# Earlier weight fetches, later scaling of omega, and bfloat16 norm matmuls in a random-feature attention with a bilinear network behind it

## The chip, the cores and the metric

The kernel runs on one core of one Trainium2 chip. The metric is device time in microseconds; the kernel before took 866.14 us (median of 3 runs, 863.68 to 867.47). A profiled execution of the same program is read below.

## The reference

q, k and v have 8 batches, 8 heads, 576 tokens and 64 columns; omega is 128 x 64. With x scaled by 64 to the power -1/4, the feature map is

```python
proj = einsum('bhsd,md->bhsm', x, omega)
h = proj - sum(x * x, -1) / 2
phi = exp(h - max(h, -1)) / sqrt(128)
```

Then kv = sum over tokens of phi(k) times v, z = sum of phi(k), and the attention's output is phi(q) kv / (phi(q) z + 1e-6). Its 4608 tokens of 512 columns go through out = (((x w1) * (x w2)) w3) w_out, with w1 and w2 of 512 x 1024, w3 of 1024 x 1024 and w_out of 1024 x 512. The four weights arrive as float64.

## The kernel before, in words

The tokens are cut into 36 chunks of 128. For a chunk of k, `features` (L258) projects it with omega on TensorE (PE) into two PSUM banks, VectorE (DVE) takes the maximum over the features (L295), ScalarE (ACT) makes the exponentials, and `in_parts` splits the result into two float16 halves. The first 9 chunks of k and the first 5 of q are projected as float32, straight from the loaded chunk and omega ("whole"); later chunks are first scaled by a power of two and split into float16 halves, and are multiplied with omega's own scaled halves. `kv_batch` sums features times v over the chunks of a batch; `q_chunk` and `q_attend` do the same for q, with a transpose by DMA between; `gate` and `project_out` are the network, with w3 w_out multiplied out once beforehand into one matrix W (`W_block`, L562).

Powers of two come from a sum of squares over a whole tile. ACT squares and sums each row; `power_of_two` (L162) adds the 128 rows by a matmul with a matrix of ones, so that every row holds the sum, and DVE takes the exponent. This matmul is called a norm here. Norms stand for omega ("om"), for each step's chunk of q and of k together ("q_k", later "q" alone), for each batch of v and for W. Omega's norm and split (L200 to L206) come at the head of the program, behind omega's two loads. The `om` halves and `unom` that they make are read from chunk 9 of k and chunk 5 of q on.

A weight goes in units through five stages: `fetch` (a DMA of 1 MB, issued on ACT's queue, L486) into one of three raw buffers of the arena, `magnitude` (ACT takes the absolute value of the high words, L494) into one of two buffers, `bits` (four DVE instructions, L500 to L504, which make float32 from float64), and, by kind, a product of PE with a copy by ACT, or a sum of magnitudes. `ORDER` gives the units: "ooWWWW11a22b..." are two units of w_out, four products of w3 with it, then w1 and w2. The stages of successive units are skewed by one tick each.

What stands where is written out as a plan of slots: each slot takes `PER[t]` ticks of the weight pipeline, one unit of the network's queue, and the functions put there by `put(slot, rank, fn)`, by rank; chunk i of q and chunk i + 5 of k begin at slot `begin[i]`, three slots each, from slot 3 on. So k's chunk 0 is projected in slot 3, behind three ticks in slot 0 and one each in slots 1 and 3. The planner of the tile framework takes this order as priority: on each engine and queue it issues what is ready by its own estimate, earlier traced work first; each engine then executes its own list in order. Loads of k, q and v and the stores stand in SyncE's (SP's) queue, weight fetches in ACT's.

Of the kernel before, what the change touches and what calls it, by code (L numbers as in the profile page):

```python
# [9 lines left out]
F32 = mybir.dt.float32  # L10
F16 = mybir.dt.float16
BF16 = mybir.dt.bfloat16
I32 = mybir.dt.int32
U32 = mybir.dt.uint32
AF = mybir.ActivationFunctionType
ALU = mybir.AluOpType
# [3 lines left out]
P = 128  # L20
# [32 lines left out]
EARLY = 6  # L53
KV_LAG = 5
K_LATE = 8
RAW64_BUFS = 3
O_BUFS = 2
RAW_BUFS = 2
# [10 lines left out]
def tile_favor_attention_then_bilinear_ffn(  # L69
# [19 lines left out]
    nc = tc.nc  # L89
# [12 lines left out]
    SCALE = 1.0 / math.sqrt(math.sqrt(D))  # L102
    TOK = GROUP * P

    const = ctx.enter_context(tc.tile_pool(name="const", bufs=1))
# [16 lines left out]
    make_identity(nc, ident)  # L122
    ones_bf = const.tile([P, P], BF16, name="ones_bf")
    nc.vector.memset(ones_bf, 1.0)
    ones = const.tile([P, P], F32, name="ones")
    nc.vector.memset(ones, 1.0)
    ln_e = const.tile([P, 1], F32, name="ln_e")
    nc.vector.memset(ln_e, 15 * math.log(2.0))

# [22 lines left out]
    def square_sum(out, src, name, pre=1.0):  # L152

        n = src.shape[1] * (src.shape[2] if len(src.shape) > 2 else 1)
        junk = at.tile([P, 512], BF16, tag="junk", name=f"junk_{name}", bufs=1)
        r0, rows = 0, src.shape[0]
        dst = junk[r0 : r0 + rows, 0:n]
        if len(src.shape) > 2:
            dst = dst.rearrange("p (i j) -> p i j", i=src.shape[1])
        nc.scalar.activation(dst, src, AF.Square, scale=pre, accum_out=out)  # L160

    def power_of_two(cols, n, name, pre=1.0, add=False, bufs=4):  # L162

        bank = bank_m(f"norm_{name}")
        nc.tensor.matmul(bank[:, 0:n], ones, cols, start=True, stop=True)
        t = bank[:, 0:n]
        if add:
            total = small("total")
            nc.vector.tensor_reduce(total, t, AX.X, ALU.add)
            t, n = total, 1  # L170

        q = bank[:, 16 : 16 + n]
        p = bank[:, 32 : 32 + n]

        nc.vector.tensor_scalar(
            q.bitcast(I32), t.bitcast(I32), 24, 23, ALU.logical_shift_right, ALU.logical_shift_left
        )
        nc.vector.tensor_scalar(p, q, 2.0**50 / pre, 2.0**-77 / pre, ALU.mult, ALU.max)
        s = small(f"s{n}_{bufs}", n, bufs=bufs)
        nc.vector.reciprocal(s, p)  # L180
        return p, s
# [13 lines left out]
    om_raw = Wb[:, 0, 0:M]  # L195
    nc.sync.dma_start(om_raw[0:D], omT)
    nc.sync.dma_start(om_raw[D:P], omT)
    om = const.tile([P, 2, M], F16, name="om")
    om_sq = const.tile([P, 1], F32, name="om_sq")
    square_sum(om_sq, om_raw, "om")  # L200
    pom, som = power_of_two(om_sq, 1, "om")
    nc.scalar.mul(om[:, 0], om_raw, som)
    nc.vector.scalar_tensor_tensor(om[:, 1], om_raw, som, om[:, 0], ALU.mult, ALU.subtract)

    unom = const.tile([P, 1], F32, name="unom")
    nc.vector.tensor_scalar_mul(unom, pom, SCALE)  # L206

    def chunks_of(b):

# [5 lines left out]
    def load(src, c, name):  # L215
        t = at.tile([P, NP, P], F32, tag=f"{name}raw", name=f"{name}raw_{c}", bufs=RAW_BUFS)
        nc.sync.dma_start(t, src[c])
        raws[name, c] = t
# [39 lines left out]
    def features(c, name):  # L258


        if whole(c, name):
            raw, es = raws.pop((name, c)), SCALE
        else:
            hl, es = hls.pop((name, c))
        pg = banks(f"{name}pj_{c}").rearrange("p g (i m) -> p g i m", m=M)
        pj = pg.rearrange("p g i m -> p (g i) m")

        def project(first=None):
            for i in range(NP):
                if first is not None:  # L270
                    for g in range(2):
                        nc.tensor.matmul(pg[:, g, i], ident, first(g * NP + i), start=True, stop=False)
                if whole(c, name):
                    for g in range(2):
                        d = slice(g * D, (g + 1) * D)
                        nc.tensor.matmul(  # L276
                            pg[:, g, i], raw[d, i], om_raw[d], start=first is None, stop=True
                        )
                    continue
                for n, (x, y) in enumerate(PASSES):  # L280
                    for g in range(2):
                        d = slice(g * D, (g + 1) * D)
                        nc.tensor.matmul(  # L283
                            pg[:, g, i],
                            hl[d, x, i],
                            om[d, y],
                            start=first is None and n == 0,
                            stop=n == len(PASSES) - 1,
                        )

        project()
        if whole(c, name) and c + 2 < NCH:
            load(srcs[name], c + 2, name)
        nm = small("nm", H)
        nc.vector.tensor_reduce(nm, pj, AX.X, ALU.max, negate=True)  # L295
        e = at.tile([P, H, M], F32, tag="e", name=f"{name}e_{c}", bufs=2)
        kind = pick(DK if name == "k" else DQ, c)
        if kind == "2":

            project(lambda h: nm[:, h : h + 1].broadcast_to([P, M]))  # L300
            nc.scalar.activation(e, pj, AF.Exp, scale=es, bias=ln_e)
        elif kind == "1":

            nc.vector.tensor_scalar(nm, nm, es, 15 * math.log(2.0), ALU.mult, ALU.add)
            for h in range(H):
                nc.scalar.activation(e[:, h], pj[:, h], AF.Exp, scale=es, bias=nm[:, h : h + 1])
        else:
            nc.vector.tensor_tensor(e, pj, nm.unsqueeze(2).broadcast_to([P, H, M]), ALU.add)  # L308
            nc.scalar.activation(e, e, AF.Exp, scale=es, bias=ln_e)  # L309
        return e  # L310
# [9 lines left out]
    ek, vhl, vraw, pv, kvs = {}, {}, {}, {}, {}  # L320

    def k_chunk(c):
        e = features(c, "k")
        ek[c] = at.tile([P, 2, H, M], F16, tag="ek", name=f"ek_{c}", bufs=EK_BUFS)
        in_parts(ek[c], e, pick(EH, c), pick(EL, c))

    def v_load(c):
        vraw[c] = at.tile([P, H, D], F32, tag="vraw", name=f"vraw_{c}", bufs=VRAW_BUFS)
        nc.sync.dma_start(vraw[c], v[c])

    vam, sv = {}, {}

# [135 lines left out]
        return free.pop(0)  # L468

    left = {}  # L470

    def used(at):

# [4 lines left out]
    def from_float64(new, src, name):  # L478

        st = {}  # L480

        def fetch():
            at = st["at"] = raw_at.pop(0)
            raw = arena[:, at : at + 4].bitcast(U32).rearrange("p b i -> p (b i)")

            nc.scalar.dma_start(raw.rearrange("p (j i) -> p j i", j=src.shape[1]), src)  # L486
            st["raw"] = raw.rearrange("p (i t) -> p i t", t=2)

        def magnitude():

            at = st["mag"] = mag_at.pop(0)
            st["g"] = arena[:, at : at + 2].rearrange("p b i -> p (b i)")
            st["dst"] = new()
            nc.scalar.activation(st["g"], st["raw"][:, :, 1].bitcast(F32), AF.Abs)  # L494

        def bits():
            g = st["g"]
            top, low = st["raw"][:, :, 1], st["raw"][:, :, 0]

            nc.vector.tensor_scalar(g, g, F64_TOP, F64_LEAST, ALU.min, ALU.max)  # L500
            g = g.bitcast(U32)
            nc.vector.tensor_scalar(g, g, 3, 0x3FFFFFFF, ALU.logical_shift_left, ALU.bitwise_and)
            nc.vector.scalar_tensor_tensor(g, top, 0xC0000000, g, ALU.bitwise_and, ALU.bitwise_or)  # L503
            nc.vector.scalar_tensor_tensor(  # L504
                st["dst"].bitcast(U32), low, 29, g, ALU.logical_shift_right, ALU.bitwise_or
            )
            raw_at.append(st["at"])
            mag_at.append(st["mag"])

        return [fetch, magnitude, bits]  # L510
# [203 lines left out]
    units, seen = [], {}  # L714
    for ch in ORDER:
        n = seen.get(ch, 0)
        seen[ch] = n + 1
        st = make[ch](n)
        units.append([None] * 3 + st + [None] if len(st) == 1 else st + [None] * (5 - len(st)))
    behind = sorted(range(5), key=lambda k: -SKEW[k])  # L720
    ticks = [
        [units[t - SKEW[k]][k] for k in behind if 0 <= t - SKEW[k] < len(units) and units[t - SKEW[k]][k]]
# [17 lines left out]
    def put(slot, rank, fn):  # L740
        plan.setdefault(slot, []).append((rank, len(plan[slot]) if slot in plan else 0, fn))
# [65 lines left out]
        step(i)  # L807
    for c in range(2):
        load(kT, c, "k")
    put(begin[-1] - 3, 11, lambda: load(qT, 0, "q"))  # L810
    put(begin[-1] - 2, 11, lambda: load(qT, 1, "q"))
    for t in range(max(plan) + 1):
        n = min(PER[t] if t < len(PER) else 1, len(ticks))
# [9 lines left out]
        n = max([1] + [-(-(k + 1) // max(due[b] - t, 1)) for k, (b, _) in enumerate(v_work)])  # L823
# [43 lines left out]
```

## Time and profile before

| | |
|---|---|
| median of 3 runs | 866.14 us |
| profiled execution, its own time | 866.7 us |
| span in the profile | 865.0 us |
| PE busy | 789.3 us (91%) |
| DVE busy | 594.4 us (69%) |
| ACT busy | 455.0 us (53%) |
| POOL busy | 222.0 us (26%) |
| chain that ended last, by engine | PE 81%, DVE 8%, DMA 4%, ACT 4%, issue 2% |
| mean DMA rate | 102 GB/s |

Busy time is the union of an engine's instructions; PEld is TensorE's weight load, which overlaps PE. The chain is the work followed back from the last instruction, at each step to what released it. A line number is that of the kernel before. The shares are averages over a beginning, in which engines wait for each other, and a long stretch in which PE is full, so they are read by stretch below.

### The profile page before, as it was taken

To read this page: it belongs to the slowest core of one execution; us is meant where nothing else is said; L and a number is where in the kernel's file an instruction comes from. 1 tells how busy PE (TensorE), PEld (TensorE's weight loads), DVE (VectorE), ACT (ScalarE), POOL (GpSimd) and SP (SyncE) were. 2 spreads that over 40 slices of the span, in tenths; PEclk is the share of its full clock that TensorE was granted. 3 is DMA by queue.
4 is the path that set the end of the run, shared out by engine and by line. 5 is a ranking of instruction groups with operands and counts; after the bars stand their busy time and mean duration, and the time that the engine had idled before them with its cause. 6 is when DMAs were issued, how large, how long until landed. Compare 5 with 4: busy or idle time off the path is not lost.

```text
span 865.0 us, 20229 instructions
## 1 busy us (share of the span) xinstructions
PE 789.3 (91%) x8479; PEld 585.1 (68%) x8484; DVE 594.4 (69%) x1066; ACT 455.0 (53%) x813; POOL 222.0 (26%) x220
## 2 busy tenths in 40 slices
PE   2876399489996899999999999999999999999998
PEld 2344255387875777777777777877777777777774
DVE  5778887887879877777877777778777754652200
ACT  2667566758456665655565656555655443322221
POOL 0000010222333433334333334343333342222110
PEclk9996599699998999999999999999999999999999
DMA  8455646432444643644534434335342343332100
GB/s 328 150 191 164 196 129 190 119 59 62 87 112 102 96 115 95 98 75 98 123 86 87 111 98 99 74 89 133 87 87 62 62 80 81 63 62 49 37 14 36
DMA packets 142522, 88.40 MB, mean 102 GB/s; under 512 B 116704, under 2 KB 116832, under 8 KB 142432
## 3 DMA queue, kind: packets, MB, share of 16 engines
q1 hardware_dynamic: 134944, 66.15, 33.7%
q10 hardware_dynamic: 7488, 20.97, 7.3%
q8 instruction: 66, 1.08, 0.5%
q14 instruction: 24, 0.20, 0.1%
HBM read 49.35 MB, written 9.44 MB: 68 GB/s over the span
## 4 chain that ended last, share of the span: by engine, by line
PE 81%; DVE 8%; DMA 4%; ACT 4%; issue 2%; POOL 0%; SPq 0%; ACTq 0%; DVEq 0%
PE ab L636 40%; PE o L665 20%; PE wp L576 7%; PE nu L401 3%; PE kvp L366 3%; PE qpj L283 2%; PE kpj L283 2%; DMA kraw<-kT 1%; DVE nm L295 1%; DMA eqT<-eq 1%; PE wp L574 1%; DMA qraw<-qT 1%; DVE w12b L504 1%; DVE arena L503 1%; PE kpj L276 1%
## 5 line engine op out<-in xcount | busy, mean ns | idle before, releaser
L636 PE MATMUL ab<-xT,w12b 128*128 128x256 f16 (+1 forms) x3840 | 396.0, 263 | 10.4 <-DMA xT<-xhl 7.1
L636 PEld LDWEIGHTS <-w12b 128*128 128x128 f16 x3840 | 342.7, 99 | 51.7 <-issue 9.0
L665 PE MATMUL o<-Wb,arena 128*128 128x512 f16 x864 | 193.6, 379 | 1.1 <-DVE Wb L146 0.6
L651 POOL TENSOR_TENSOR arena<-asb,arena 128x512 f16<-128x512 f32 x72 | 84.5, 1174 | 294.9 <-ACT arena L650 294.4
L665 PEld LDWEIGHTS <-arena 128*128 128x128 f16 x864 | 84.3, 100 | 94.6 <-issue 1.5
L318 POOL TENSOR_TENSOR eq<-qe,eq 128x1024 f16<-128x1024 f32 x34 | 73.9, 2172 | 141.2 <-DVE eq L132 86.8
L646 DVE TENSOR_TENSOR asb<-ab,asb 128x512 f32<-128x512 f32 x72 | 49.4, 687 | 62.9 <-PE ab L636 62.5
L650 ACT CAST arena<-asb 128x512 f16<-128x512 f32 x72 | 44.3, 615 | 85.5 <-DVE asb L646 85.5
L318 POOL TENSOR_TENSOR ek<-ke,ek 128x1024 f16<-128x1024 f32 x28 | 59.7, 2131 | 103.2 <-ACT ek L134 62.2
L576 PE MATMUL wp<-w12b 128*128 128x512 f32 x128 | 60.9, 631 | 13.5 <-DVE w12b L504 13.5
L309 ACT ACTIVATE qe<-qe,ln_e,es 128x1024 f32<-128x1024 f32 x31 | 38.4, 1240 | 47.6 <-DVE qe L308 47.6
L146 DVE SCALAR_TENSOR_TENSOR khl<-kraw,s,khl 128x512 f16<-128x512 f32 x27 | 49.3, 1827 | 16.2 <-ACT khl L143 16.2
L576 PEld LDWEIGHTS wp<-w12b 128*128 128x128 f32 x128 | 25.6, 203 | 45.7 <-issue 31.3
L309 ACT ACTIVATE ke<-ke,ln_e,es 128x1024 f32<-128x1024 f32 x27 | 33.5, 1241 | 42.9 <-DVE ke L308 42.9
L146 DVE SCALAR_TENSOR_TENSOR qhl<-qraw,s,qhl 128x512 f16<-128x512 f32 x31 | 27.9, 899 | 37.7 <-ACT qhl L143 37.7
L401 PEld LDWEIGHTS <-eqT 128*128 128x128 f16 (+1 forms) x960 | 32.4, 101 | 29.0 <-DMA eqT<-eq 19.4
L401 PE MATMUL nu<-kv,eqT 128*128 128x65 f16 (+1 forms) x960 | 34.8, 196 | 18.5 <-DMA eqT<-eq 18.5
L160 ACT ACTIVATE junk_q<-qraw 128x512 bf16<-128x512 f32 x31 | 19.5, 630 | 60.4 <-DMA qraw<-qT 60.4
L645 ACT ACTIVATE asb<-ab 128x512 f32<-128x512 f32 x72 | 42.0, 584 | 16.1 <-PE ab L636 11.0
L437 ACT ACTIVATE xhl<-xs,p2r 128x512 f16<-128x512 f32 x36 | 25.9, 719 | 41.1 <-DVE p2r L189 40.1
L295 DVE TENSOR_REDUCE nm<-kpj 128x8 f32<-128x1024 f32 x36 | 43.8, 1217 | 3.6 <-PE kpj L276 3.3
L132 DVE CAST eq<-qe 128x1024 f16<-128x1024 f32 x31 | 21.5, 693 | 34.2 <-ACT qe L309 34.2
(127 smaller groups left out, 996.2 us busy)
## 6 DMA issues: line engine op xcount, KB each, us to landing
kraw<-kT SPq DMA_DIRECT2D x36, 256.0 KB, 2.7
vraw<-v SPq DMA_DIRECT2D x36, 256.0 KB, 3.5
qraw<-qT SPq DMA_DIRECT2D x36, 256.0 KB, 2.7
out<-o SPq DMA_DIRECT2D x36, 256.0 KB, 2.2
arena<-w3T ACTq DMA_DIRECT2D x8, 1024.0 KB, 5.2
arena<-w ACTq DMA_DIRECT2D x8, 1024.0 KB, 6.0
arena<-wo ACTq DMA_DIRECT2D x4, 1024.0 KB, 6.1
eqT<-eq SPq DMA_TRANSPOSE x72, 3.1
```

The lines of the kernel that those rows point to most:

```text
L146: nc.vector.scalar_tensor_tensor(lo, src, s, hi, ALU.mult, ALU.subtract)
L295: nc.vector.tensor_reduce(nm, pj, AX.X, ALU.max, negate=True)
L309: nc.scalar.activation(e, e, AF.Exp, scale=es, bias=ln_e)
L318: (nc.vector if lo == "d" else nc.gpsimd).tensor_tensor(t[:, 1], e, t[:, 0], ALU.subtract)
L401: nc.tensor.matmul(nu[r0:r1, h // 4, h % 4], t[:, x, place(h), r0:r1], kvs[b][:, y, h], start=n == 0, stop=n == 2,)
L576: nc.tensor.matmul(ps, w[:, j, k * P : (k + 1) * P], guest[:, j], start=j == j0, stop=j == HALF - 1,)
L636: nc.tensor.matmul(ps[:, k], w12[m][i][cc][:, a, r * P : (r + 1) * P], x[:, b, cc, off : off + T], start=j == 0, stop=j == len(mm) - 1,)
L645: nc.scalar.mul(asb, ab[0], 2.0**-37)
L646: nc.vector.tensor_tensor(asb, ab[1], asb, ALU.mult)
L650: nc.scalar.copy(h[:, 0], asb)
L651: nc.gpsimd.tensor_tensor(h[:, 1], asb, h[:, 0], ALU.subtract)
L665: nc.tensor.matmul(ps, hs[c, f][0][:, a], W[f][:, b], start=i == 0, stop=i == len(mm) - 1)
```

## The change

Five edits. (1) The `fetch` stage of the first three weight units is called ahead of the plan, and ahead of k's loads, and left out of its ticks. (2) Omega's square, norm and split become a function `om_split`, put in slot 11 with rank 4. (3) The load of v's chunk 0 gets a dependency with a semaphore on the last DVE instruction of the first converted unit. (4) What `features` traces on DVE for chunk 0 of k is issued behind the last DVE instruction of the second converted unit; this is an order of issue on DVE without a semaphore. (5) A norm takes the upper 16 bits of each float32 sum as bfloat16 and multiplies with a bfloat16 matrix of ones; the float32 matrix of ones and its memset go.

```diff
+OM_AT = 11
+K_BEHIND = 1
...
-    ones = const.tile([P, P], F32, name="ones")
-    nc.vector.memset(ones, 1.0)
...
-        nc.tensor.matmul(bank[:, 0:n], ones, cols, start=True, stop=True)
+        nc.tensor.matmul(bank[:, 0:n], ones_bf, cols.bitcast(BF16)[:, 1::2], start=True, stop=True)
...
-    square_sum(om_sq, om_raw, "om")
-    pom, som = power_of_two(om_sq, 1, "om")
-    nc.scalar.mul(om[:, 0], om_raw, som)
-    nc.vector.scalar_tensor_tensor(om[:, 1], om_raw, som, om[:, 0], ALU.mult, ALU.subtract)
-
     unom = const.tile([P, 1], F32, name="unom")
-    nc.vector.tensor_scalar_mul(unom, pom, SCALE)
+
+    def om_split():
+
+        square_sum(om_sq, om_raw, "om")
+        pom, som = power_of_two(om_sq, 1, "om")
+        nc.scalar.mul(om[:, 0], om_raw, som)
+        nc.vector.scalar_tensor_tensor(om[:, 1], om_raw, som, om[:, 0], ALU.mult, ALU.subtract)
+        nc.vector.tensor_scalar_mul(unom, pom, SCALE)
...
     def k_chunk(c):
-        e = features(c, "k")
+        if c == 0:
+            with tc.issue_after(converted[K_BEHIND]):
+                e = features(c, "k")
+        else:
+            e = features(c, "k")
...
-        nc.sync.dma_start(vraw[c], v[c])
+        dma = nc.sync.dma_start(vraw[c], v[c])
+        if c == 0:
+
+            tc.add_manual_dep(
+                dma.ins,
+                converted[0].name,
+                mybir.DependencyInfo(mybir.DependencyClass.Sync, mybir.DependencyReason.DATA),
+                reason="v_load",
+            )
...
+    converted = []
...
-            nc.vector.scalar_tensor_tensor(
-                st["dst"].bitcast(U32), low, 29, g, ALU.logical_shift_right, ALU.bitwise_or
+            converted.append(
+                nc.vector.scalar_tensor_tensor(
+                    st["dst"].bitcast(U32), low, 29, g, ALU.logical_shift_right, ALU.bitwise_or
+                ).ins
             )
...
+    for u in units[:RAW64_BUFS]:
+        u[0]()
+        u[0] = None
...
     for c in range(2):
         load(kT, c, "k")
+    put(OM_AT, 4, om_split)
```

## Rows read from the trace of the kernel before

**Rows 1.** Stretches: us, busy us (x instructions) per engine, granted clock, DMA share, GB/s.

```profile
2.50:15.00 12.50, 4.98 (x34) 4.48 (x34) 4.92 (x12) 3.93 (x6) 0.00 (x0) 1.00 1.03 389
25.00:56.00 31.00, 31.00 (x80) 13.92 (x81) 22.20 (x24) 18.94 (x41) 0.00 (x0) 1.00 0.48 153
56.00:290.00 234.00, 182.16 (x2119) 133.59 (x2123) 191.96 (x333) 150.87 (x303) 43.64 (x45) 0.87 0.47 123
290.00:787.00 497.00, 497.00 (x5693) 380.57 (x5691) 351.92 (x651) 261.15 (x431) 168.06 (x152) 1.00 0.41 89
```

**Rows 2.** The chain of waits, first 60 us: start, us, what.

```profile
12.17 1.22 DVE nm L295
13.39 0.60 DVE arena L500
...
17.24 0.61 DVE arena L500
...
21.09 0.61 DVE arena L500
...
25.00 23.41 PE wp L576 x48
```

**Rows 3.** Timeline of ACT and its queue, first 25 us: start, us, what [idle before].

```profile
0.74 0.42 ACTq L486 DMA_DIRECT2D arena<-wo  x1
6.22 1.28 ACT L160 ACT_TABLE_LOAD   x1 [6.22 <-DMA Wb<-omT]
6.33 0.42 ACTq L486 DMA_DIRECT2D arena<-wo  x1
...
9.77 0.38 ACTq L486 DMA_DIRECT2D arena<-w3T  x1
9.80 1.11 ACT L494 ACTIVATE arena<-arena 128x1024 f32<-128x1024 f32 x1
```

**Rows 4.** The first three fetches in issue order: KB each, us to landing.

```profile
arena<-wo ACTq DMA_DIRECT2D x1, 1024.0 KB, 5.1
...
arena<-wo ACTq DMA_DIRECT2D x1, 1024.0 KB, 7.8
...
arena<-w3T ACTq DMA_DIRECT2D x1, 1024.0 KB, 9.4
```

**Rows 5.** Norm matmuls (L165) from 290 to 787 us: ns min/median/max, first and last start.

```profile
L165 PE MATMUL norm_q_k<-sums,ones x40: 252/262/273, 306.4 to 672.0; 128*128 128x3 f32 x40
L165 PE MATMUL norm_v<-vam,ones x10: 256/256/256, 312.5 to 659.5; 128*128 128x8 f32 x10
L165 PE MATMUL norm_q<-sums,ones x10: 171/252/273, 690.3 to 764.0; 128*128 128x3 f32 x10
```

**Rows 6.** Timeline of PE from 330 to 344 us.

```profile
336.49 0.84 PE L283 MATMUL qpj<-om,qhl 64*128 64x128 f16 x24
337.26 5.41 PE L636 MATMUL ab<-xT,w12b 128*128 128x256 f16 x48
342.61 0.84 PE L283 MATMUL kpj<-om,khl 64*128 64x128 f16 x24
...
343.63 0.38 PE L665 MATMUL o<-Wb,arena 128*128 128x512 f16 x1
```

**Rows 7.** The chain of waits at three places behind 290 us.

```profile
312.71 0.20 PE norm_v L165 x2
...
368.09 3.63 PE kvp L366 x120
...
707.96 0.12 PE norm_q L165 x2
```

**Rows 8.** Timeline of DVE, omega's first and last instruction.

```profile
8.89 0.17 DVE L175 TENSOR_SCALAR norm_om<-norm_om 128x1 int32<-128x1 int32 x1 [6.40 <-PE norm_om L165]
...
11.61 0.34 DVE L203 SCALAR_TENSOR_TENSOR om<-Wb,s,om 128x128 f16<-128x128 f32 x1
```

**Rows 9.** Timeline of PE at 96 us.

```profile
96.24 0.29 PE L401 MATMUL nu<-kv,eqT 128*128 128x65 f16 x2 [10.42 <-DMA eqT<-eq]
```

## The prediction

> **What bounds the kernel now.** I read the page's slices first, then busy time by stretch, the chain of waits, and the timelines of the places that the change touches. By stretch the kernel falls in two [rows 1]. From 290 to 787 us PE is busy in all 497.00 us, so that every nanosecond taken out of PE's order there comes off the end, while DVE works 352 of them and cannot become the bound by a few per cent. From 56 to 290 PE is busy 182.16 of 234 us; DVE, at 191.96, carries most of the chain with transposes and loads between, and 52 us of PE's idle time lie there. The first 25 us are one chain [rows 2]: k's first two chunks, their maxima, then three float64 conversions of DVE one behind the other, and only at 25.00 us PE's first product of two weights. From 25 to 56 PE is full again with these products.
>
> Why do the conversions start at 13.39 us? ACT's timeline says it [rows 3]. The first weight fetch goes out at 0.74 us, the second at 6.33 and the third at 9.77, because ACT's queue is in order and between them stand the square of omega, which waits for its load until 6.22 us, and later omega's scaling. The first fetch landed 5.1 us after its issue, at 5.84 us; the other two shared the DMA engines with k, v and q and took 7.8 and 9.4 us [rows 4].
>
> **The bfloat16 norms.** A norm is one matmul of ones in the source and two in the trace: 40 + 10 + 10 records, so 20 + 5 + 5 norms between 290 and 787 us, and 12 norms ahead of that [rows 5]. With float16 operands each matmul is one record, so I expect one record and one weight load in bfloat16. The price of one where it counts is read from starts, because modelled ends overlap [rows 6]. Without a norm, 24 projections and the step to the next full-width matmul take 337.26 - 336.49 = 0.77 us; with one, 343.63 - 342.61 = 1.02 us. The norm adds 0.25 us. A single pass with few columns should cost what the densest small float16 pairs of weight load and matmul cost: 120 of them in 3.63 us, 0.03 us each [rows 7]. Saved: 0.25 - 0.03 = 0.22 us, in the 21 norms that stand behind projections (20 joint ones and the first of q alone): 4.6 us. The 5 norms of v add 0.20 us in the chain, the other 4 of q, hidden in part behind long matmuls, 0.12 us [rows 7]: 5 x 0.17 + 4 x 0.09 = 1.2 us. Sum 5.8 us. Its ends: 6.7 us if the norm becomes free (21 x 0.25 + 5 x 0.20 + 4 x 0.12), and 3.3 us if one pass costs exactly half of two. The 12 earlier norms I take at nothing, since DVE's chain covers them; at most 11 x 0.22 = 2.4 us. The missing memset of ones runs on an idle DVE: nothing.
>
> Here a page speaks against the small price. The Trainium skill, "TensorE: Matmul & The Clock Gate", section "LDWEIGHTS (loading the stationary operand)", makes the load's time the number of columns over 1.2 GHz; for 128 columns that is an estimate of 0.107 us, which three columns of matmul cannot hide. By it the 21 norms would save about 0.14 us each, 3.0 us in place of 4.6. The trace disagrees for 16-bit weights: the 0.03 us per pair above hold a 128-column load each [rows 7]. I stay with the row.
>
> **The three fetches first.** All three leave ACT's queue from 0.74 us on, ahead of the wait for omega; the source puts them ahead of k's two loads as well, but those go out on SP's queue. The first lands near 5.84 us as before. Behind it ACT needs the table load of 1.28 us and the magnitude of 1.11 us [rows 3]; that gives 8.25 us, or 8.75 if omega's short square still comes first. I take 8.5. A conversion takes 3.85 us (13.39 to 17.24 to 21.09 to 24.95) [rows 2], so three end at 8.5 + 11.6 = 20.1 us if the data is there. Is it? DMA moved 389 GB/s from 2.5 to 15 us, with its 16 engines busy throughout (share 1.03) [rows 1]. The second block is wanted at 12.35 - 1.15 = 11.2 us: 1.05 MB at half that rate behind 5.84 us land at 11.2, and 12.8 if SP's loads (omega 0.07, k 0.52, four chunks of v 1.05, q 0.26 MB) all go ahead of it. The third is wanted at 15.05; all 5.05 MB need 13.0 us from 2.5, 15.5 us. So 0 to 1.6 us late.
>
> **k's first maximum** may stand no sooner than behind the second conversion; by the order of the source it then comes behind the third, since that conversion is traced in an earlier place. Chunk 1's maximum has no such edge and may slip into a gap. Each in front of the third conversion costs 1.3 us, 1.22 for itself [rows 2] and a little for its scaling. Product start: 20.1 us with none, 21.4 with one, 24.2 with two and late data. I take 21.0: gain 4.0 us, ends 0.8 and 5.1. Queued behind the maximum are chunk 0's exponentials on ACT, which free the bank that chunk 2's projection needs; PE comes to that one only behind the first 48 products, at 48.41 us [rows 2], some 25 us behind the maximum's new place, so it costs nothing, and DVE has 8.8 of 31 us idle from 25 to 56 [rows 1] for the maxima that move there, twice 1.3 us.
>
> **v's loads.** The wait is put on chunk 0's load alone. The planner issues what is ready, so the other four probably leave where they did, and chunk 0 waits in SP's queue until about 12.4 us, with the later loads of q and k behind it. Those loads feed work behind the first products, which end at 48.41 us [rows 2]: cost nothing. If all five waited, 1.05 MB less would compete early, which moves the start toward 20.1 only.
>
> **Omega's parts** leave a stretch where ACT and DVE waited anyway and may fall into slot 11, behind the first products, where DVE is the bound. Five instructions on DVE, 0.17 us for the first and 0.34 for the last [rows 8], about 1.0 us. The planner may also fill a gap with them: 0 to 1.0, I take 0.8, since DVE is busy 82% of that stretch (191.96 of 234) [rows 1]. Chunk 9 is the first to read them: far off.
>
> **Sum.** 5.8 + 4.0 - 0.8 = 9.0 us. The profiled execution took 866.7 us (span 865.0): 857.7. The median of the runs lies 0.6 below it, so the forecast is 857.1 us. It supposes that 56 to 290 us shifts as a whole; nothing in it waits for anything but the program itself.
>
> **Rivals.** (a) The start's 4 us is lost between 56 and 290: the planner lays every queue anew, and 52 us of PE's idle time there can grow by 4. For: DVE, ACT, PE and DMA hand over to each other in that chain, and a handover that just fitted may not fit. Against: no fixed time in it. 861.1 us. (b) One bfloat16 weight load costs as much as one float32 load, so a norm is halved and no more: 3.3 in place of 5.8 us, 859.6. For: no row of before shows a bfloat16 norm; against: the float16 pairs. The Trainium skill's rule cited above would have it so. (c) Slower: PE waited 10.42 us for the first transpose of q's features at 96.24 us [rows 9], with DVE and ACT full of conversions ahead of it. If the planner, which now has conversions earlier and k's maxima later, puts one more q chunk behind conversions, PE stands another 10.42 us, and a conversion of 3.85 us that waits behind the chunk comes on top: 857.1 + 14.3 = 871.4 us. It decides once PE's idle time before 290 us has grown by over 9 us. For: such a wait is there already; against: the order of q and k chunks is fixed by slots, which do not change. (d) The new order closes gaps there instead: 5 us more, about 852. (e) The wait on v's load does not do what it says, as argued: no change of the sum.
>
> **How the numbers follow.** Forecast 0.50 (853 to 861), (a) 0.20, (b) 0.08, (c) 0.10, (d) 0.12. A measurement of this kernel cannot tell a difference within 0.5%, 861.8 to 870.5 us, from no change. (a) lies near that edge and gives 0.08 to faster and 0.12 to no change; with the forecast, (b) and (d) faster has 0.78, same 0.12, slower 0.10. Range: the lower end takes (d) and the best ends of the norms, 850; the upper end takes (a) with norms at half, 864.
>
> **What would show it.** Right: one norm record per norm, and 24 projections to the next matmul in about 0.80 us; three fetches issued before 2.5 us; the first product at 20 to 21.5 us; idle time of PE from the first products to the full stretch within 3 us of 52. Wrong: a product start past 24 us (the fetches hindered each other), norms with two records, or PE's full stretch beginning less than 3 us earlier though the product began 4 us earlier, which is (a); beginning later than before is (c).

## The result, and the profile after

The changed kernel takes 858.52 us (median of 4 runs, 857.69 to 859.34) against 866.09 us for the kernel before on the same chip (4 runs, 863.68 to 867.47): a ratio of 0.9911, 95% interval 0.9888 to 0.9935. The forecast was 857.1 us. The total agrees with it; of the terms of its sum only the largest does. The norms gave what they were to give, and the earlier start gave almost nothing.

The changed kernel by stretch, columns as in [rows 1]:

```profile
56.00:290.00 234.00, 182.06 (x2154) 133.09 (x2153) 192.27 (x338) 151.68 (x305) 46.90 (x46) 0.86 0.49 125
290.00:787.00 497.00, 497.00 (x5687) 379.71 (x5684) 353.91 (x653) 261.13 (x430) 165.68 (x152) 1.00 0.40 90
```

Between 56 and 290 us PE works 182.06 us, as before, and is idle for 52 again. That looks like a shift as a whole, but a stretch with fixed edges cannot show it; landmarks of the work itself do (the table below).

The chain of waits of the changed kernel, first 26 us (start, us, what), beside [rows 2]:

```profile
0.74 5.58 DMA arena<-wo
...
6.34 7.96 DMA arena<-w3T
...
22.68 7.53 PE wp L593 x13
```

The first product stands at 22.68 us, 2.3 us ahead of before, not 4.0. The chain leads through the third fetch, which left at 6.34 us, 0.02 us behind the landing of the first, and landed at 14.30 us. But a chain names one of two conditions that are met at almost the same moment; DVE's timeline in the changed kernel (start, us, instruction, idle before and what ended it) says what that landing cost:

```profile
9.20 0.69 DVE L515 TENSOR_SCALAR arena<-arena 128x1024 f32<-128x1024 f32 x1 [6.84 <-ACT arena L509]
...
15.60 0.69 DVE L515 TENSOR_SCALAR arena<-arena 128x1024 f32<-128x1024 f32 x1 [0.15 <-ACT arena L509]
...
17.94 1.22 DVE L297 TENSOR_REDUCE nm<-kpj 128x8 f32<-128x1024 f32 x1
...
20.28 1.22 DVE L297 TENSOR_REDUCE nm<-kpj 128x8 f32<-128x1024 f32 x1
21.42 1.21 DVE L520 SCALAR_TENSOR_TENSOR w12b<-arena 128x1024 uint32<-128x1024 uint32 x1
```

From 9.20 us to the product DVE waits once for work, 0.15 us. It is full with three conversions and both of k's first maxima (L297), which ran ahead of the third conversion's last step (L520).

The timelines of ACT with its queue, and of SP's queue, in the changed kernel, beside [rows 3]:

```profile
0.74 0.98 ACTq L501 DMA_DIRECT2D arena<-wo  x2
6.34 0.37 ACTq L501 DMA_DIRECT2D arena<-w3T  x1
6.75 1.28 ACT L509 ACT_TABLE_LOAD   x1 [6.75 <-DMA arena<-wo]
8.04 1.12 ACT L509 ACTIVATE arena<-arena 128x1024 f32<-128x1024 f32 x1
```

```profile
3.25 1.00 SPq L219 DMA_DIRECT2D qraw<-qT  x2
...
14.34 3.35 SPq L335 DMA_DIRECT2D vraw<-v  x5
```

Two fetches, not three, went out at once, and all five of v's loads went behind the first conversion, not chunk 0's alone.

The norms of the changed kernel from 290 to 787 us (ns min/median/max, first and last start), beside [rows 5], with their weight loads:

```profile
L165 PEld LDWEIGHTS <-ones_bf x30: 95/96/99, 303.0 to 754.9; 128*128 128x128 bf16 x30
L165 PE MATMUL norm_q_k<-sums,ones_bf x20: 177/178/178, 303.0 to 663.7; 128*128 128x3 bf16 x20
L165 PE MATMUL norm_v<-vam,ones_bf x5: 171/171/171, 309.0 to 651.5; 128*128 128x8 bf16 x5
L165 PE MATMUL norm_q<-sums,ones_bf x5: 167/168/178, 681.9 to 755.0; 128*128 128x3 bf16 x5
```

Thirty records in place of sixty. And their price by starts, in PE's timeline of the changed kernel, beside [rows 6]:

```profile
332.52 0.84 PE L285 MATMUL qpj<-om,qhl 64*128 64x128 f16 x24
333.30 5.41 PE L653 MATMUL ab<-xT,w12b 128*128 128x256 f16 x48
338.64 0.84 PE L285 MATMUL kpj<-om,khl 64*128 64x128 f16 x24
339.42 0.18 PE L165 MATMUL norm_q_k<-sums,ones_bf 128*128 128x3 bf16 x1
339.46 5.34 PE L682 MATMUL o<-Wb,arena 128*128 128x512 f16 x24
```

Without a norm 0.78 us from the projections to the next matmul, with one 0.82 us: a norm now adds 0.04 us where it added 0.25.

**Where the time came from.** Starts of PE's instructions, in us, in one profiled execution of each kernel (the second group are the experiments below). "Sums 24" is the last of the 24 sums (nu) of q's chunk 0, "gate 1" and "gate 1000" the first and the thousandth matmul of the gate (ab), "last o" the end of the last output matmul:

| kernel | first product | kvp 120 | first nu | sums 24 | gate 1 | gate 1000 | last o | median of runs |
|---|---|---|---|---|---|---|---|---|
| before | 25.00 | 82.95 | 96.24 | 103.66 | 122.07 | 298.41 | 861.16 | 866.09 |
| after | 22.68 | 81.68 | 94.96 | 102.59 | 121.23 | 295.05 | 852.14 | 858.52 |
| after_again | 22.23 | 80.53 | 93.81 | 103.19 | 121.96 | 298.43 | 855.52 | 859.70 |
| after_third | 22.55 | 81.89 | 95.17 | 102.66 | 121.42 | 298.18 | 855.27 | 860.04 |
| norms_only | 24.37 | 81.86 | 95.15 | 102.72 | 120.98 | 294.43 | 851.52 | 860.42 |
| norms_again | 24.40 | 82.14 | 95.40 | 103.16 | 121.38 | 294.61 | 851.70 | 859.73 |
| front_only | 22.28 | 81.42 | 94.72 | 102.37 | 120.91 | 294.63 | 857.40 | 864.98 |
| no_k_edge | 27.50 | 85.74 | 98.27 | 103.80 | 121.86 | 298.11 | 855.20 | 858.11 |
| both_behind_third | 20.20 | 81.76 | 95.04 | 102.74 | 121.22 | 294.48 | 851.57 | 857.70 |
| both_and_table | 20.23 | 79.86 | 93.13 | 102.69 | 121.68 | 297.87 | 854.94 | 859.93 |
| om_slot5 | 22.36 | 80.92 | 94.19 | 104.26 | 123.31 | 296.78 | 853.87 | 859.25 |
| v_free | 25.79 | 79.55 | 93.89 | 100.62 | 118.34 | 291.41 | 848.51 | 855.48 |
| hold | 22.92 | 81.77 | 95.06 | 98.65 | 117.68 | 293.95 | 851.03 | 854.86 |
| hold_early | 20.33 | 81.16 | 94.45 | 98.03 | 116.91 | 290.78 | 847.85 | 853.95 |

Three columns carry the story. From gate 1000 to the last o the kernel before takes 562.75 us and each of the kernels with bfloat16 norms 557.07 to 557.10; front_only, with float32 norms, takes 562.77. So 5.66 us is the norms' share in the full stretch, and no other edit changes it. Ahead of it, the changed kernel's 2.3 to 2.8 us at the first product have shrunk to 0.1 to 0.8 us at gate 1 (three profiles); the kernels with the norms alone, without the earlier start, gain 0.7 and 1.1 us there. Between gate 1 and gate 1000 a difference of 3 us comes and goes between executions of one and the same kernel (173.82, 176.47 and 176.76 us in the three of the changed kernel); that is treated with after_again.

### The profile page after: what moved, and what is told of

It is laid out like the page before. It is cut to its first block, busy times and chain, and to the rows that moved or that the text cites. A ratio compares the mean times of both kernels' runs of the same rounds, so it can differ in the third digit from the quotient of the medians.

```text
span 855.9 us, 20148 instructions
## 1 busy us (share of the span) xinstructions
PE 781.3 (91%) x8442; PEld 576.2 (67%) x8442; DVE 593.8 (69%) x1065; ACT 455.2 (53%) x813; POOL 221.7 (26%) x220
## 4 chain that ended last, share of the span: by engine, by line
PE 81%; DVE 8%; DMA 4%; ACT 3%; issue 2%; POOL 0%; SPq 0%; ACTq 0%; DVEq 0%
PE ab L653 41%; PE o L682 20%; PE wp L593 6%; PE nu L415 3%; PE kvp L380 3%; PE qpj L285 3%; PE kpj L285 2%; DVE nm L297 2%; DVE vhl L146 1%; DMA arena<-w3T 1%; DMA eqT<-eq 1%; DVE arena L518 1%; DMA kraw<-kT 1%; PE qpj L278 1%; PE wp L591 1%
## 5 line engine op out<-in xcount | busy, mean ns | idle before, releaser
L682 PEld LDWEIGHTS <-arena 128*128 128x128 f16 x864 | 82.2, 98 | 94.7 <-issue 1.8
L297 DVE TENSOR_REDUCE nm<-kpj 128x8 f32<-128x1024 f32 x36 | 43.8, 1217 | 5.0 <-PE kpj L278 4.9
```

The lines of the kernel that those rows point to most:

```text
L682: nc.tensor.matmul(ps, hs[c, f][0][:, a], W[f][:, b], start=i == 0, stop=i == len(mm) - 1)
```

## The experiments

Median times are compared with the kernel before on the same chip: 867.24 us for the first four, 867.61 for the next four, 865.38 for the last four.

### norms_only and front_only: the change in two halves

norms_only is the kernel before with the bfloat16 norm; front_only is the changed kernel with the float32 norm.

```diff
-        nc.tensor.matmul(bank[:, 0:n], ones, cols, start=True, stop=True)
+        nc.tensor.matmul(bank[:, 0:n], ones_bf, cols.bitcast(BF16)[:, 1::2], start=True, stop=True)
```

> The kernel before with the bfloat16 norms alone; omega, the fetches and k's maxima stay as they were. Theory (the two halves add up: norms save 21 x 0.203 + 5 x 0.194 + 4 x 0.114 = 5.7 us by the starts in the trace after, and the start of the program gives the rest): 5.7 us under before, 860.4 us, with the first product of two weights still at 25.0 us and 24 projections to the next matmul in 0.82 us. Rival (the gain is mostly that of the earlier start, and shorter norms are given back to waits between 56 and 290 us): less than 3 us under before. Second rival (the planner lays the queues anew for the shorter norms and closes gaps): over 7 us.

> The kernel after with the float32 norms and their matrix of ones: the earlier fetches, omega's parts in slot 11, the wait of v's load and the edge of k's first maximum alone. Theory (halves add up): 3.4 us under before, 862.7 us: the landmark of the first joint norm behind projections was 3.37 us earlier in the trace after, and only three norms of it lie on the chain ahead of that. First product at 22.7 us. Rival (the start is taken back between 56 and 290 us, what looked like it was norms): within 1 us of before, though the first product starts at 22.7 us.

Measured: norms_only 860.42 us, ratio 0.9912 (0.9879 to 0.9944); front_only 864.98 us, ratio 0.9982 (0.9961 to 1.0003). The norms alone reach the changed kernel's ratio; the start alone is 2.3 us in the medians, told apart neither from nothing nor from the 3.4 expected. The 6.8 us of norms_only are 5.66 in the full stretch and some 1.1 ahead of gate 1 (122.07 to 120.98 in the table), with an interval wide enough for either.

### no_k_edge and both_behind_third: the first product moved by 7 us

```diff
-        if c == 0:
-            with tc.issue_after(converted[K_BEHIND]):
-                e = features(c, "k")
-        else:
-            e = features(c, "k")
+        e = features(c, "k")
```

both_behind_third goes the other way: `if c <= 1:` with `K_BEHIND = 2`, so that both maxima stand behind the third conversion.

> The kernel after without the edge that puts chunk 0's maximum behind the second conversion. In DVE's list both maxima then stand ahead of all three conversions, though k's loads now land later. Theory (DVE is busy without a gap from the first magnitude at 9.2 us on, so the order alone decides): the maxima wait for k's projections, which began at 9.9 us, and end near 15.0 us; three conversions of 3.85 us follow, first product at 26.5 us, later than the 25.0 us of before: 3.8 us over the kernel after, 862.3 us. Rival (both maxima stand ahead of the first product in the kernel after as well, so the edge is worth nothing): product at 22.7 us, 858.5 us.

> The kernel after with the edge moved: the maxima of k's chunks 0 and 1 stand behind the third conversion. Theory (the two maxima that got ahead of the third conversion's end are what my start of 21.0 us lacked, 2 x 1.2 us): first product at 20.3 us, 2.3 us under the kernel after, 856.2 us. Rival (exponentials of chunks 0 and 1 come later and the stretch from 56 us on waits for them, or a handover there swallows it): product at 20.3 us, total 858.5 us as after. Third (DVE stands waiting for the third magnitude, whose block landed at 14.3 us and takes 1.2 us on ACT): product not before 21.5 us, 857.3 us.

Measured: no_k_edge 858.11 us, ratio 0.9897 (0.9865 to 0.9929); both_behind_third 857.70 us, 0.9890 (0.9858 to 0.9923). both_behind_third's start came as expected (20.20 us against 20.3), no_k_edge's a microsecond later (27.50 against 26.5), and no_k_edge's total not at all (862.3 expected). The total of both_behind_third lies between theory and rival (856.2 and 858.5). The timeline of PE in no_k_edge, and behind it in both_behind_third (start, us, instruction, idle before and what ended it):

```profile
27.50 2.93 PE L589 MATMUL wp<-w12b 128*128 128x512 f32 x3 [10.39 <-DVE w12b L516]
...
98.27 0.29 PE L411 MATMUL nu<-kv,eqT 128*128 128x65 f16 x2 [9.33 <-DMA eqT<-eq]
...
102.65 1.39 PE L411 MATMUL nu<-kv,eqT 128*128 128x65 f16 x22 [2.94 <-DMA eqT<-eq]
```

```profile
20.20 9.97 PE L593 MATMUL wp<-w12b 128*128 128x512 f32 x16 [6.90 <-DVE w12b L520]
...
95.04 0.29 PE L415 MATMUL nu<-kv,eqT 128*128 128x65 f16 x2 [10.42 <-DMA eqT<-eq]
...
101.60 1.39 PE L415 MATMUL nu<-kv,eqT 128*128 128x65 f16 x22 [4.68 <-DMA eqT<-eq]
```

The start differs by 7.30 us, the first sums by 3.23, the other 22 sums by 1.05, and gate 1 by 0.64. PE waits twice for transposes of q's features there, and the second wait, 2.94 against 4.68 us, takes up most of what had been left. But of the 7.30 us, 3.3 had gone ahead of both transposes: kvp 120 differs by 3.98. The edge on k's maximum is worth nothing in total that can be told, in either direction.

### after_again and norms_again: what an execution alone does

> The kernel after once more, on one chip with the kernel before and with the next one. Theory (what the earlier start gains is largely spent between the 64th product, 3.2 us early in the trace after, and the first sum of k times v, 1.3 us early; PE's full stretch then starts 1 to 2 us early): 7 to 8 us under before on this chip, 1 to 2 us under the norms alone. Rival (the start carries through whole): 3.4 us under the norms alone.

> The kernel before with bfloat16 norms alone, once more, beside the kernel after. Theory: 5.7 to 6.5 us under before, and 1 to 2 us over the kernel after. Rival (the start carries through whole): 3.4 us over the kernel after. Second rival (nothing of the start is left): within 0.5 us of the kernel after.

Measured: 859.70 us, ratio 0.9918 (0.9893 to 0.9944), and 859.73 us, 0.9917 (0.9887 to 0.9946). With the float32 norms exchanged, the rest of the change is worth nothing that can be told: norms_again lies within 0.1 us of after_again, as its second rival had it, and not the expected 1 to 2 us above. The pair of profiles of the one changed kernel shows two places where executions part. The first is the load of a chunk of q in the chain of waits, in after and then in after_again:

```profile
185.42 2.84 DMA qraw<-qT
```

```profile
186.17 5.01 DMA qraw<-qT
```

From gate 200 to gate 400 the first takes 18.6 us and the second 20.9; the kernel before took 20.1, with 4.4 us for that load, norms_only and norms_again 18.4 and 18.2. So of the 9.0 us between the profiles of before and after some 1.5 us are this load (2.5 us lie between gate 1 and gate 1000 as a whole), and single profiles should not be compared across it. The second is six float32 transposes of PE, in the timelines of after and of after_again:

```profile
73.59 4.59 PE L591 MATMUL wp<-Wb,ident 128*128 128x512 f32 x6
```

```profile
73.80 3.23 PE L591 MATMUL wp<-Wb,ident 128*128 128x512 f32 x6
```

The granted clock from 72 to 80 us was 0.67 in the one and 0.83 in the other, behind a stretch (64 to 72 us) at 0.50, 1.2 GHz, in both, where PE was busy 3.31 and 3.09 of 8 us. PE has next to no idle time from there to the sums of k, so this is why kvp 120 stands at 80.53 us in after_again, 1.15 us earlier than in after. But the sums 24 come at 103.19, 0.6 us later than in after: the gain was lost at the second transpose.

### om_slot5 and both_and_table: more time ahead of the transposes

om_slot5 puts omega's parts into slot 5 (`OM_AT = 5`). both_and_table is both_behind_third with ACT's table loaded while the first fetch is under way:

```diff
     nc.vector.memset(ln_e, 15 * math.log(2.0))
+    warm = const.tile([P, 1], F32, name="warm")
+    nc.scalar.activation(warm, ln_e, AF.Abs)
```

> The kernel after with omega's square, norm and split in slot 5 in place of slot 11. DVE then does its five instructions among the first products, where it stands idle 6.7 us of 30. Theory (in slot 11 they stand in DVE's chain behind the products, 54.8 to 57.0 us, and cost about 1 us there, with 1.6 us in which DVE waited for the norm): first kvp sum ends 1 us or more earlier than after's 81.7 us, total 1.0 us under the kernel after. Rival (DVE's list is only reordered; the next wait takes the microsecond): same as after within 0.5 us.

> The kernel after with both of k's first maxima behind the third conversion, and one small activation at the head so that ACT's table load (1.28 us, behind the first fetch in the trace after) runs while the first fetch is under way. Theory (the start is spent downstream): first product at 19.0 us, 3.7 us ahead of after, but the first kvp sum no more than 1 us ahead, total 0 to 1 us under after. Rival (start carries through): 3.7 us under after.

Measured: om_slot5 859.25 us, ratio 0.9903 (0.9878 to 0.9927); both_and_table 859.93 us, 0.9903 (0.9874 to 0.9932). Neither is told apart from the changed kernel, and om_slot5's kvp 120, 80.92 us, lies between those of the changed kernel's own profiles. both_and_table's kvp 120 is 1.8 us ahead of after's, where at most 1 was expected, and its total has none of it. The table load moved as meant, but the product came at 20.23 us, not at 19.0. ACT's and DVE's timelines in both_and_table say why:

```profile
6.43 1.12 ACT L511 ACTIVATE arena<-arena 128x1024 f32<-128x1024 f32 x1 [3.74 <-DMA Wb<-omT]
9.24 1.12 ACT L511 ACTIVATE arena<-arena 128x1024 f32<-128x1024 f32 x1 [1.68 <-DMA arena<-wo]
```

```profile
7.58 0.69 DVE L517 TENSOR_SCALAR arena<-arena 128x1024 f32<-128x1024 f32 x1 [5.23 <-ACT arena L511]
...
10.39 0.69 DVE L517 TENSOR_SCALAR arena<-arena 128x1024 f32<-128x1024 f32 x1 [1.39 <-ACT arena L511]
```

The first conversion starts 1.6 us earlier than in the changed kernel, but the second one's data is late: its magnitude waits 1.68 us for the second fetch, and DVE stands for 1.39 us. Of the transposes: in both_and_table the second left at 92.46 us, 1.9 us earlier than in both_behind_third (94.35), and landed 9.04 us later instead of 7.20. What the start had gained up to there was gone when it landed.

### hold, hold_early, v_free and after_third: the second transpose

Behind the second transpose of q's chunk 0 two weight fetches of 1 MB leave within 1.2 us; in every kernel so far they share the DMA engines with it. hold makes these two (HOLD, blocks 5 and 6 of w3) wait for the transpose, whose instruction is the last in the list `turned`:

```diff
-            nc.scalar.dma_start(raw.rearrange("p (j i) -> p j i", j=src.shape[1]), src)
+            dma = nc.scalar.dma_start(raw.rearrange("p (j i) -> p j i", j=src.shape[1]), src)
+            if name in HOLD:
+                tc.add_manual_dep(
+                    dma.ins,
+                    turned[-1].name,
+                    mybir.DependencyInfo(mybir.DependencyClass.Sync, mybir.DependencyReason.DATA),
+                    reason="hold",
+                )
```

hold_early is the same on both_and_table. v_free is the changed kernel without the dependence of v's load on the first conversion:

```diff
-        if c == 0:
-
-            tc.add_manual_dep(
-                dma.ins,
-                converted[0].name,
-                mybir.DependencyInfo(mybir.DependencyClass.Sync, mybir.DependencyReason.DATA),
-                reason="v_load",
-            )
```

after_third is the changed kernel once more.

> The kernel after with two weight fetches (blocks 5 and 6 of w3) held until the second transpose of q's chunk 0 has landed. In the traces so far the two transposes left between 89.9 and 94.8 us and the second landed between 101.5 and 103.1 us whatever the start did: 9.7 us behind the first one's issue in after, 11.5 in after's second profile, 7.8 where the fetches came 0.6 us behind it. Theory (the transpose shares the DMA engines with the two fetches of 1 MB that go out as it does, and that is where a start is evened out): the second transpose lands 2 us or more sooner, the sums of q's chunk 0 end near 100 us; the fetches land later by as much or more, and since their conversions feed the next product, the first gate starts at 121 to 122 us as before: total as after, within 1 us. Rival (the transpose is slow by itself): it still takes 7 us and more from its issue.

> The same two fetches held, in the kernel with both maxima behind the third conversion and the early table load, whose first product came at 20.2 us. Theory (without the fetches beside it the transpose lands a fixed time behind its issue, so an earlier start shows there): q's chunk 0 sums about 0.7 us ahead of those of the run before, as its kvp sums were. Total between 857 and 860 us. Rival (something else fixes the place): the same time as in the run before.

> The kernel after without the wait of v's first load. All five loads of v then stand ahead of q's in SP's list and go out from 3 us on, beside the fetches. Theory: 1.3 MB more share the DMA engines early, first product 1 to 1.5 us later than after's 22.2 to 22.7 us; nothing of that is left at the first gate (121 to 122 us), total as after within 1 us. Rival (the wait is worth what the start loses): total 1 to 1.5 us over after.

> The kernel after on the same chip as the three runs before, for comparison and for a third profile: product start at 22.2 to 22.7 us, q's chunk 0 sums ending at 102 to 104 us, 7 to 8 us under the kernel before.

Measured: after_third 860.04 us, ratio 0.9939 (0.9923 to 0.9955); hold 854.86 us, 0.9882 (0.9864 to 0.9899); hold_early 853.95 us, 0.9872 (0.9855 to 0.9889); v_free 855.48 us, 0.9890 (0.9868 to 0.9911). hold was expected within 1 us of after_third and came 5.2 us below it; v_free likewise, and came 4.6 below. hold_early came 3 us below the lower end expected, and after_third gained 5.3 us on the kernel before, not 7 to 8. PE's timeline in after_third and the weight fetches on ACT's queue there:

```profile
95.17 0.29 PE L415 MATMUL nu<-kv,eqT 128*128 128x65 f16 x2 [10.41 <-DMA eqT<-eq]
...
101.51 1.39 PE L415 MATMUL nu<-kv,eqT 128*128 128x65 f16 x22 [4.46 <-DMA eqT<-eq]
```

```profile
94.61 0.40 ACTq L501 DMA_DIRECT2D arena<-w3T  x1
...
95.63 0.37 ACTq L501 DMA_DIRECT2D arena<-w3T  x1
```

The same of hold:

```profile
95.06 0.29 PE L418 MATMUL nu<-kv,eqT 128*128 128x65 f16 x2 [10.42 <-DMA eqT<-eq]
...
97.50 1.39 PE L418 MATMUL nu<-kv,eqT 128*128 128x65 f16 x22 [0.57 <-DMA eqT<-eq]
```

```profile
97.48 0.37 ACTq L505 DMA_DIRECT2D arena<-w3T  x1
...
97.89 0.52 ACTq L505 DMA_DIRECT2D arena<-w3T  x1
```

And the landing times of the two transposes, in after_third and in hold:

```profile
DMA to landing us min/median/max: 3.2/5.1/7.0
```

```profile
DMA to landing us min/median/max: 3.1/3.2/3.2
```

Both kernels reach the first sums at the same moment (95.17 and 95.06 us). Without the fetches both transposes take 3.1 to 3.2 us; beside them the second takes 7.0. With that, PE's wait falls from 4.46 to 0.57 us, and gate 1 comes at 117.68 us instead of 121.42, although the fetches left 2.3 to 2.9 us later. The Trainium skill, "DMA: Bandwidth & Descriptors", section "Queues, rings and completion order", says that a DMA engine takes turns between the queues that have work for it, a packet at a time; the trace agrees so far as the transpose on SP's queue takes 2.2 times as long beside the fetches on ACT's.

That the early start counts again once this wait is away is not shown: hold_early, whose product comes 2.6 us earlier than hold's, is 0.8 us earlier at gate 1 and 0.9 us in the medians, within the intervals. Of the 2.6 us, 2.0 are gone at kvp 120, ahead of both transposes. Its median is the lowest of all, 0.9872 of the kernel before and below the changed kernel's; it is not told apart from hold and v_free.

v_free is the surprise. Its product comes 3.2 us later than after_third's, and yet it is ahead from kvp 120 on. SP's queue in v_free:

```profile
3.29 4.23 SPq L335 DMA_DIRECT2D vraw<-v  x5
```

ACT's first work with its queue there:

```profile
9.65 0.37 ACTq L493 DMA_DIRECT2D arena<-w3T  x1
10.05 1.28 ACT L501 ACT_TABLE_LOAD   x1 [10.05 <-DMA kraw<-kT]
```

and PE's timeline there:

```profile
49.32 7.13 PE L585 MATMUL wp<-w12b 128*128 128x512 f32 x16
...
68.90 1.22 PE L278 MATMUL qpj<-Wb,qraw 64*128 64x128 f32 x6 [0.94 <-ACT ke L308]
...
99.47 1.39 PE L407 MATMUL nu<-kv,eqT 128*128 128x65 f16 x22 [4.14 <-DMA eqT<-eq]
```

The loads go out as before the change, and the first product is nearly as late as there, less for the bytes that they add than for ACT's queue: the third weight fetch left only at 9.65 us, when a load of k had landed, and ACT's table load and first magnitude (11.35 us against 8.04 in after) stood behind it. What v_free gains lies elsewhere. From the 49th product of w3 and w_out, the first of the last 16, to q's first projection it takes 19.6 us. The same two places in after and in both_behind_third:

```profile
46.26 7.13 PE L593 MATMUL wp<-w12b 128*128 128x512 f32 x16
...
69.34 1.22 PE L278 MATMUL qpj<-Wb,qraw 64*128 64x128 f32 x6 [1.89 <-ACT ke L308]
```

```profile
44.93 7.13 PE L593 MATMUL wp<-w12b 128*128 128x512 f32 x16
...
69.71 1.22 PE L278 MATMUL qpj<-Wb,qraw 64*128 64x128 f32 x6 [2.75 <-ACT ke L308]
```

That is 23.1 and 24.8 us. And the second transpose leaves at 92.33 us, 2.2 us earlier than in after_third (94.49), and takes about as long (7.09 us), so that it lands earlier. From 56 to 80 us DVE ran 47 instructions against 36, and PE's granted clock was 0.79 against 0.64. So the wait on v's load is not free. Which part of DVE's and ACT's new order shortens that stretch, and what share the clock has, was not separated, and hold with v_free was not run.

## Why the prediction was right or wrong

**The norms: right.** One record per norm, as expected. In starts a norm adds 0.04 us behind projections against 0.03 forecast; 5.8 us were summed, and gate 1000 to the end gained 5.66. Rival (b), a norm only halved, would have given 3.3 us and is out. The rule weighed there (the Trainium skill, "TensorE: Matmul & The Clock Gate", section "LDWEIGHTS (loading the stationary operand)", an estimate of 0.107 us for 128 columns) gives the load's time, not the price of one: the bfloat16 load's own record is 96 ns long, near that estimate, but PE's order grew by only 0.04 us, so most of the load lay beside other work. The prediction set a load's time against the spacing of pairs, which are two things. The 12 earlier norms, taken at nothing, were worth at most about 1 us (norms_only at gate 1: 1.09, norms_again 0.69).

**The first product: direction right, size wrong.** It came at 22.68 us, not 21.0, 2.3 us gained of 4.0. The terms that missed: the first conversion began at 9.20 us, not at 8.5, because the first fetch landed 0.5 us later (6.32 us) and the table load came 0.4 us behind it, since ACT issued the third fetch in between; and k's first maximum did not come "behind the third" conversion. It ran as soon as the second was done (17.94 us), and chunk 1's ran ahead of the third's last step too, so that two maxima of 1.14 us from start to start, not one at most, stood in the way. both_behind_third takes both out and starts at 20.20 us (its first conversion began at 8.62). "All three leave ACT's queue from 0.74 us on" failed as well: the third left when the first had landed. By the trace, the program's first eight DMAs have eight semaphores, and the third fetch, the ninth, has the one that the first used. Two runs gave it another, and the wait moved with it: in both_and_table it waited for omega's load and left at 6.01 us, in v_free for a load of k and left at 9.65. In the changed kernel it cost the 0.4 us just named and no more, for the landing at 14.30 us lies within the bounds of the prediction, and DVE waited 0.15 us.

**The step that failed** is "It supposes that 56 to 290 us shifts as a whole", with which the start entered the sum at 4.0 us. This is rival (a), given 0.20, and it was true of the start: in the eleven profiles without held fetches and without v_free the first product stands anywhere from 20.2 to 27.5 us, and gate 1 within 120.9 to 123.3. The rival's own reason, a handover that just fitted, was too vague. The start is spent in three places, in us:

| kernel | product 49 to q's first projection | from there to kvp 120 | second transpose, issue to landing |
|---|---|---|---|
| before | 22.23 | 11.29 | 6.91 |
| norms_only, norms_again | 22.24, 22.24 | 11.13, 11.21 | 7.06, 7.22 |
| after, after_again, after_third | 23.08, 23.07, 23.08 | 12.34, 10.99, 12.46 | 7.12, 8.86, 6.97 |
| om_slot5 | 22.98 | 12.19 | 9.54 |
| both_behind_third, both_and_table | 24.78, 24.63 | 12.05, 11.50 | 7.20, 9.04 |
| hold, hold_early | 23.08, 24.64 | 12.30, 11.90 | 3.09, 3.07 |
| v_free | 19.57 | 10.65 | 7.09 |

The first column is the same to 0.01 us in all profiles of the two kernels that have more than one, so it goes with the order of the work and not with the execution. (front_only has 23.38 us there; in no_k_edge the order is another.) The change made it 0.85 us longer, both maxima behind the third conversion another 1.6 to 1.7, and without the wait on v's load it is 3.5 us shorter than in the changed kernel. DVE is full there (12.97 of 13.00 us from 56 to 69 us in after); which instructions make the difference is not shown. The second column is PE's own work, with at most 0.4 us of idle time, and here executions of one kernel differ: the 1.35 us between after and after_again are the six transposes at two granted clocks. In the profile of after these two places take 1.9 of the 2.3 us that it loses between product 49 (3.2 us ahead of before) and gate 1 (0.84).

The third place is the one that hold isolates: the second transpose of q's chunk 0, 3.1 us by itself, is stretched to 6.3 to 9.5 by two fetches that leave with it. In the eleven profiles it left anywhere from 92.5 to 96.3 us and landed between 101.2 and 103.1; in after_again 2.0 us of the start are lost there, in after 0.2. Why the landing hardly moves is not shown, and in v_free it did move, to 99.42 us. [rows 9] shows the first of the two waits; the second stood right behind it in the kernel before:

```profile
102.51 1.39 PE L401 MATMUL nu<-kv,eqT 128*128 128x65 f16 x22 [4.39 <-DMA eqT<-eq]
```

I did not ask why one of two equal transposes was more than twice as late as the other.

**Omega's parts** at 0.8 us: om_slot5, which moves them again, is not told apart from the changed kernel, so the term is not confirmed and not refuted: it shortens the first column above by 0.1 us, and kvp 120 and the total changed by less than executions differ. **v's loads**: rival (e) was wrong, the dependence does what it says and for all five loads, and the cost that I put at nothing is 4.6 us in the medians (v_free against after_third), more than the start was to gain.

**Why the total still came out.** Forecast 5.8 + 4.0 - 0.8 = 9.0 us. Measured 5.66 in the full stretch and 0.1 to 0.8 ahead of gate 1, while the medians of three comparisons gained 7.6, 7.9 and 5.3 us; the rest is what executions differ by. Between the two profiles the sum was met to 0.1 us by chance: 9.0 us are 5.66 in the full stretch, 0.84 ahead of gate 1 and 2.5 between gate 1 and gate 1000, where the changed kernel's own profiles differ by 2.9. So its closeness is luck in part: differences between executions stood in for a start that was worth next to nothing. That it held at all is the norms' doing, which alone (860.42 us) lie in its range. Rival (c), one more transpose wait, did not occur, but it named waits for these transposes, which hold then showed to be worth several microseconds.

**What would have shown it** was named in part: the sign of (a), a late stage that gains less than the product, is there, with PE's first gate 0.84 us earlier and the product 2.3. The sign of being right, 52 us of idle time between 56 and 290 us, was there as well and did not tell the two apart.

## What to carry to other kernels

A gain at the start counts only as far as the next place that does not move with it, so follow it landmark by landmark (here first product, kvp, first sums, gate) instead of adding it to the end, and ask of each wait for a DMA what else the DMA engines carry at that moment. Two equal transfers with unequal landing times, 3.2 and 7.0 us here, are the sign; holding back the neighbour that is not urgent was worth more than moving the start. An edit that only clears the way has a price of its own: the wait on v's load cost 4.6 us, which only the run that leaves it out showed. Compare several executions before a difference of 3 us in a single profile is explained.

## What was not expected of the hardware

- A DMA transpose of q's features lands 3.1 to 3.2 us after its issue alone and 6.3 to 9.5 us beside two fetches of 1 MB.
- A load of 256 KB took 2.84 us in one execution and 5.01 in another of the same kernel.
- Six float32 matmuls of 128x512 took 3.23 or 4.59 us in two executions of the same kernel, at a granted clock of 0.83 and 0.67 over the 8 us around them.
- One bfloat16 norm costs 0.04 us in PE's order where the float32 one, with two records and two weight loads, cost 0.25.
